# Small copies, minima and products placed on GpSimd, two-channel table products, dense products ahead of score steps, and plain first loads in a fused attention and state-space kernel

## The chip, the cores and the metric

The kernel runs on one core of a Trainium2 chip. The metric is the device time of one execution in microseconds (us); the median over the runs is compared. An execution that the hardware profiler recorded lies beside it: its span runs from the first to the last recorded instruction, and its own time is a little longer than its span.

## The reference, cut to what matters

```python
# A: 2048 tokens in 4 segments of 512, 32 heads of 16
q, k, v = x @ wq, x @ wk, x @ wv
for s in range(4):                                   # segment by segment
    p = softmax(qs @ ks.T / 4 + causal_mask)         # local attention
    a_mem = phi(qs) @ M / (phi(qs) @ z + 1e-6)       # phi(t) = t+1 if t>0 else exp(t)
    o = g * a_mem + (1 - g) * (p @ vs)
    M += phi(ks).T @ vs;  z += phi(ks).sum()
a = o @ wo
# B: a diagonal state-space convolution, 512 channels, 128 states
K[d, l] = Re(sum_n C[d,n] * exp(dt[d] * A[d,n] * l) * dt[d] * B[d,n])   # A, B, C complex
b = causal_convolution(x, K) + x * Dskip             # through FFTs in the reference
out = g_tok * a + (1 - g_tok) * b                    # g_tok = sigmoid(x . gate_w)
```

## The kernel before

Everything is recorded first as a list of operations with their readers and writers. A planner (`Sched.schedule`) then places them, engine by engine, with a cost for each operation and a priority (`key`, shifted for each group of operations by the table `ORDER`). Some operations, above all the evacuations of PSUM, may go to ScalarE or VectorE: the planner chooses, and the choice is fixed in the program. Each engine runs its list strictly in the order that comes out; waits are on semaphores. DMAs stand in SP's list, a few large ones in GpSimd's. All matmuls are issued from one helper (L820), all evacuations from another (ScalarE L324 and L327, VectorE L325 and L328), all DMAs from a third (L317).

**Part A, attention.** For each of 4 segments, `do_xT` brings the 512 tokens transposed into SBUF (DMA transposes); `project` makes q and k for 8 heads at a time (128 rows), evacuates them, makes a copy of k in which even heads are zeroed (`ko`, L1121), and, from the second segment on, phi(q): exp on ScalarE (L1125), then a minimum with 1, a maximum with 0, and a sum on VectorE (L1126 to L1128). `seg_state` does the same for k after a transpose on TensorE (exp L1075, maximum L1076, minimum L1077, sum L1078) and adds to the memory. `group` does 4 heads in five score steps: two or four matmuls write 1024 columns over two PSUM banks, ScalarE takes the exp of them (L1169, 160 times in all), and a matmul with v follows. The two bank pairs (0, 1) and (2, 3) are used in turn. The causal mask of a step is either added on TensorE (two matmuls with the identity) or multiplied in on VectorE after the exp (L1178); the table `MASKS` says which, bit by bit. `ophase` normalises (L1229 to L1252), sends the result through DRAM for a transpose, and `oproj` multiplies by wo.

**Part B, the convolution.** The kernel K is needed at 640 exponents, each a sum of one of 20 values (F) and one of 32 (G). `ssm_prep` makes exp(dt·A); `ssm_powers` squares it nine times in fp32, and at each of the 10 powers, for two halves of the channels, stores (re, im) in bf16, a negated im (L904) and a second copy of re (helper, 128x256). `tables(c)` builds F and G for 128 channels by complex products `cmul` (VectorE: L1328 and L1330 the two products, L1333 their sum), starting from five copies of 256 elements; `n` is the number of entries made at once, 1 to 8, so 256 to 2048 elements. It then multiplies G by F on TensorE channel by channel: 256 matmuls of 20 columns with 32-column weights for each c, 1024 in all, two evacuations of 320 elements for each c, and four small DMAs into the table KTT. `x_level1` makes the first step of the transform of x and stores it in DRAM (`scr_Z`).

**The tail.** 16 steps, each with 10 dense matmuls of KTT with a DFT matrix (loaded by GpSimd's queue), the second step of the transform of x, four VectorE operations for the complex product (L1425 to L1430), the way back, and a DMA into V2. It can begin only when the four tables are done, and the planner mixes it with the last groups of the attention. At the end 16 blocks of three matmuls, evacuated with the token gate (L327, L328), are written out.

**First loads.** SP issues six DMA transposes first (A_re, A_im, four parts of x), while ScalarE's queue issues the identity, log_dt, wq and wk.

Of the kernel before, what the change touches and what calls it, by code (L numbers as in the profile page):

```python
# [16 lines left out]
    'c_ident': (-302.654696, 118.5323), 'c_mk': (25.0776717, 31.1201), 'c_negm': (117.240337, 15.88946),  # L17
    'c_mask': (82.9696732, 148.73681), 'c_ones': (219.06097, 69.01982), 'c_W1': (101.972009, -1.91191),
    'c_G2': (152.510402, 64.12832), 'ld0': (-159.6066, -3.90904), 'ld1': (-178.483329, -24.17737),
    'ld2': (-92.104013, -32.87557), 'ld3': (-67.6677276, 9.94046), 'ld4': (-16.8975543, -9.33976),  # L20
    'ld5': (-4.87843354, -20.81767), 'ldt': (-255.221528, 18.97994), 'ldw0.3': (-120.015437, 20.25449),
    'ldw0.4': (-107.069287, 54.02795), 'ldw0.5': (-74.7706898, 55.68128), 'ldw50': (143.580885, 71.64248),
    'ldbd': (146.873282, -3.63178), 'ldc': (75.9548493, -139.44835), 'prep': (241.088944, 76.53782),
    'xT0': (-135.794939, 94.16918), 'powA0': (-118.34783, 47.94242), 'powA1': (293.056234, 56.59733),
    'powA2': (35.605867, 26.1545), 'powA3': (85.9672701, 3.55388), 'powA4': (-134.9878, 64.48103),
    'powA5': (-26.1625064, 59.29796), 'powA6': (-133.006553, -36.0664), 'powA7': (-142.410857, 92.25773),
    'powA8': (-143.096642, 54.65219), 'powA9': (-10.832777, 2.7911), 'cbA': (-135.566534, 76.23563),
    'powB0': (-38.6484402, 86.47076), 'powB1': (5.73197339, 19.09463), 'powB2': (-13.5842481, 50.52935),
    'powB3': (-134.626625, -55.3453), 'powB4': (-158.321758, -62.26012), 'powB5': (-189.375726, 81.95324),
    'powB6': (-80.3854645, -2.33938), 'powB7': (-23.5296877, 39.40937), 'powB8': (-69.1011372, 80.90111),  # L30
    'powB9': (-110.631611, 11.18354), 'cbB': (-43.7416241, -8.34436), 'gate0': (-83.6885532, -16.32166),
    'gate': (1.11235274, 54.68591), 'proj0.0': (-19.4170356, -12.54463), 'tok0': (-79.3938344, 28.87985),
    'state0': (2.03704365, 1.9988), 'grp0.0.0': (-9.77190791, 56.39033), 'grp0.0.1': (-15.5684214, 42.32006),
    'oph0.0': (16.6476846, 20.40017), 'proj0.1': (-31.4882721, 74.16452), 'grp0.1.0': (-22.0475879, 127.40729),
    'grp0.1.1': (-23.8762151, 61.87469), 'oph0.1': (-9.68776635, -98.76067), 'proj0.2': (13.8209713, 33.73148),
    'grp0.2.0': (-3.0729207, -42.9295), 'grp0.2.1': (-4.41502647, 85.93088), 'oph0.2': (-0.110628858, -73.44253),
    'proj0.3': (-3.65051527, 62.72309), 'grp0.3.0': (-157.898249, 69.86549), 'grp0.3.1': (15.8097506, 82.05476),
    'oph0.3': (1.58288994, 45.63335), 'oproj0': (-119.328043, -32.2024), 'xT1': (152.351944, 17.87594),
    'proj1.0': (9.25225381, 119.56925), 'tok1': (-10.2534902, 33.782), 'state1': (2.65910208, -104.20105),
    'grp1.0.0': (-90.77533, -81.81367), 'grp1.0.1': (2.11773201, -114.61486), 'oph1.0': (-2.73170943, -41.40325),  # L40
    'proj1.1': (1.88542876, 58.71674), 'grp1.1.0': (-50.654272, 32.17712), 'grp1.1.1': (2.9233842, 75.51506),
    'oph1.1': (-10.8350984, -95.48593), 'proj1.2': (1.82372045, 0.09674), 'grp1.2.0': (-40.190034, 101.48513),
    'grp1.2.1': (6.26606409, 118.92692), 'oph1.2': (-0.686318884, -116.61307), 'proj1.3': (0.240651948, 30.33776),
    'grp1.3.0': (-46.8631087, 31.58558), 'grp1.3.1': (4.26113506, 92.65595), 'oph1.3': (16.5142754, -29.00959),
    'oproj1': (-191.3713, -3.8356), 'xT2': (96.7803542, 126.17717), 'proj2.0': (2.03309827, 56.77169),
    'tok2': (4.1651971, -119.61949), 'state2': (5.77674239, -0.78865), 'grp2.0.0': (-34.2653109, -9.07765),
    'grp2.0.1': (-5.67836684, 97.22657), 'oph2.0': (-250.752907, -56.23876), 'proj2.1': (6.5976729, 122.63846),
    'grp2.1.0': (-4.50294478, 30.38303), 'grp2.1.1': (4.81855669, 106.57043), 'oph2.1': (15.6722872, -167.79793),
    'proj2.2': (-0.107249989, 90.02738), 'grp2.2.0': (-195.487509, 48.11696), 'grp2.2.1': (-5.26881311, 86.02262),
    'oph2.2': (10.7493513, -113.28868), 'proj2.3': (-7.49951321, 95.76044), 'grp2.3.0': (5.83724795, 81.21215),  # L50
    'grp2.3.1': (-32.6003357, 74.62712), 'oph2.3': (-34.0930078, -105.98926), 'oproj2': (-42.4160159, -7.99807),
    'xT3': (290.268696, 20.01374), 'proj3.0': (0.804501688, 7.58942), 'tok3': (5.05705523, 9.43832),
    'grp3.0.0': (-16.6209468, 115.71971), 'grp3.0.1': (-94.3400298, 75.95984), 'oph3.0': (34.3743725, -53.14357),
    'proj3.1': (-5.34871522, 74.39357), 'grp3.1.0': (31.8837621, -11.25205), 'grp3.1.1': (-311.171354, -14.40604),
    'oph3.1': (-107.203104, -69.86356), 'proj3.2': (72.9991952, 27.09956), 'grp3.2.0': (20.1657102, -6.85936),
    'grp3.2.1': (-59.0699755, -14.4919), 'oph3.2': (88.4879918, -147.86965), 'proj3.3': (79.119397, 97.40507),
    'grp3.3.0': (5.32990942, 126.86441), 'grp3.3.1': (61.7741135, -22.60438), 'oph3.3': (-130.287319, -60.50239),
    'oproj3': (-33.6345043, -45.3022), 'tab0': (-0.0762501383, 297.60803), 'tab1': (-3.85305439, 267.74954),
    'tab2': (-0.288638216, 266.94455), 'tab3': (9.72332812, 324.53498), 'xl1': (-134.058337, -22.9888),
    'tailload': (-94.6594205, 59.19368), 'K0': (-16.3376241, 5.32994), 'K1': (44.0845545, -26.15755),  # L60
    'K2': (9.34286849, 3.42233), 'K3': (45.356053, 32.70617), 'K4': (39.7158986, -80.36254),
    'K5': (59.226848, -13.36243), 'K6': (-175.798043, 23.12264), 'K7': (-52.4250027, -83.01271),
    'K8': (-81.0202091, -26.97997), 'K9': (70.2758069, 29.6753), 'K10': (11.2349379, 25.06385),
    'K11': (-5.3357892, -30.98575), 'K12': (-72.5533468, 4.35854), 'K13': (83.6417633, 0.11429),
    'K14': (94.4918388, -109.55134), 'K15': (132.562985, 53.83523), 'fin': (-85.9153477, -15.31372),
    'pre0': (169.976104, -25.42423), 'fin0': (91.9347751, 60.72191), 'pre1': (-73.3504102, -61.54381),
    'fin1': (115.799027, 117.99035), 'fin2': (125.104546, 66.48059), 'fin3': (213.962257, 170.74892),
}
MASKS = [2, 0, 0, 0, 0, 0, 0, 0, 0, 28, 0, 0, 0, 1, 0, 0, 16, 16, 14, 4, 0, 28, 0, 1, 3, 15, 31, 31, 15, 13, 26, 20]
# [122 lines left out]
class Sched:  # L192
# [141 lines left out]
    def schedule(self):  # L334
# [23 lines left out]
        dma_free = 4.5  # L358
# [221 lines left out]

def c_mm(n, k=1):
    return k * (0.014 + n / 2300.0)
# [53 lines left out]
def dft_const():  # L636
    lq = (np_bf16_bits(np.arange(2048, dtype=np.float32)).astype(np.uint32) << 16).view(np.float32).astype(np.int64)
    where = {}
    for f, fe in enumerate(F_EXP):
        for g, ge in enumerate(G_EXP):  # L640
            assert fe + ge not in where
            where[fe + ge] = (f % 5, 4 * g + f // 5)
# [14 lines left out]
def build_kernel(nc, A_x, A_wq, A_wk, A_wv, A_wo, A_beta, B_A_re, B_A_im, B_B_re, B_B_im,  # L657
                 B_C_re, B_C_im, B_log_dt, B_Dskip, gate_w, out):
    with contextlib.ExitStack() as es:
# [102 lines left out]
        kexP = mkpool("kex", 1280, 2)  # L762
# [3 lines left out]
        assert a <= 207 * 1024, a  # L766

        pbP = mkpool("pb", 1024, 2)
# [9 lines left out]
        pb2P = mkpool("pb2", 1024, 1, 0)  # L778
        a = GP.addr
        paP = mkpool("pa", 1024, 2, 0)  # L780
# [44 lines left out]
        for wi in range(6):  # L825
            T = Tile(paP if wi < 2 else pb1P if wi == 2 else pb2P if wi == 3 else pbP, BF16)
            S.tag = "ld%d" % wi
            S.dma(lambda T=T: ap(T, n=512), lambda wi=wi: bass.AP(prm[wi], 0, [[128, 512], [1, 128]]), 131072, w=[T], key=(-1.6, -1.7, 3.0, 3.1, 3.2, 3.3)[wi], tr=True)
            praw.append(T)
# [3 lines left out]
        for T, wsrc, ky in ((wqT, A_wq, 0.3), (wkT, A_wk, 0.4), (wvT, A_wv, 0.5), (woT, A_wo, 50.0)):  # L833
            S.tag = "ldw%g" % ky
            S.dma(lambda T=T: ap(T, dims=[[512, 4], [1, 512]]), lambda wsrc=wsrc: wsrc.rearrange("(k p) n -> p k n", p=128),
                  524288, w=[T], key=ky - 1.3 if ky < 1 else ky, early=ky < 0.45)
# [15 lines left out]
        def do_xT(s):  # L852
            S.tag = "xT%d" % s
            T = Tile(xTP, BF16)
            parts = []
            for k in range(4):
                S.dma(lambda T=T, k=k: ap(T, k * 512, n=512), lambda k=k: bass.AP(x.tensor, x.offset + s * 262144 + k * 128, [[512, 512], [1, 128]]),
                      131072, pw=[T], key=S.key - 8 if s else -1.5 + 0.1 * k, tr=True)
# [714 lines left out]
```

## Time and profile before

| what | value |
|---|---|
| median of 3 runs | 357.27 us (355.72 to 368.35) |
| the profiled execution's own time | 355.81 us |
| its span | 354.0 us |
| ScalarE busy | 285.9 us, of it 157.5 us the 160 exps |
| VectorE busy | 274.6 us, of it 101.4 us the table products (L1328, L1330, L1333) |
| TensorE busy | 298.4 us (ends of matmuls are modelled) |
| GpSimd busy | 17.3 us |
| mean granted TensorE clock | 0.946 of full speed |

In a row of the groups stand the line, engine and operation, then what is written and read with its shape, the count, the busy time and the mean of one, and the idle time of the engine just before. In a row of the stages stand, for each engine, busy time and number of instructions, then the granted clock, the busy share of the DMA engines and what they moved. "issue" as a releaser is time in which an engine waited for nothing that the profile shows. Lines of the changed file stand some 5 to 50 further down than those named here.

### The profile page before, as it was taken

Reading aid. Unit: us, or ns where it says so; the run is one execution under the profiler, and the core shown is the slowest. Engines: PE = TensorE matmul, PEld = TensorE weight load, DVE = VectorE, ACT = ScalarE, POOL = GpSimd, SP = SyncE. Lnnn points to the kernel's source line nnn. Section 1 sums busy time; section 2 is a strip of 40 time slices with the busy share of each in tenths; the row PEclk is TensorE's granted clock in tenths of the full one; section 3 lists DMA queues with packets and bytes.
Section 4 is the critical chain, followed back from the end, with each engine's and each line's share of the span. In section 5 each row is a group of like instructions: output and inputs, shape, how many; then the busy total and the mean of one; then the engine's idle time right before and its main releaser. Section 6 shows DMA issues by size and latency. Waiting matters only on the chain.

```text
span 354.0 us, 8296 instructions
## 1 busy us (share of the span) xinstructions
PE 298.4 (84%) x3409; PEld 125.1 (35%) x3409; DVE 274.6 (78%) x667; ACT 285.9 (81%) x387; POOL 17.3 (5%) x39
## 2 busy tenths in 40 slices
PE   0669887688939999999889999987999999999691
PEld 0223332233424432543335543353343333344240
DVE  2788999999848998399998899942877778986220
ACT  2798999899937998998999898945999768665472
POOL 2000000000000000000010000000001120100000
PEclk9996999699987996999999999998999999999897
DMA  7879021013592474801006210251134656533342
GB/s 173 172 161 109 1 91 30 3 54 99 197 148 76 136 176 126 205 23 30 2 8 186 71 44 17 59 167 37 40 102 181 217 181 211 149 114 93 109 156 90
DMA packets 43117, 37.56 MB, mean 106 GB/s; under 512 B 30568, under 2 KB 35944, under 8 KB 42216
## 3 DMA queue, kind: packets, MB, share of 16 engines
q1 hardware_dynamic: 39016, 22.18, 25.8%
q0 software_dynamic: 2720, 13.63, 12.3%
q10 hardware_dynamic: 1344, 1.21, 1.5%
q8 instruction: 27, 0.44, 0.5%
q14 instruction: 10, 0.08, 0.1%
HBM read 17.74 MB, written 9.44 MB: 77 GB/s over the span
## 4 chain that ended last, share of the span: by engine, by line
DVE 38%; PE 33%; ACT 20%; issue 4%; DMA 3%; SPq 0%
PE psum L820 33%; ACT sb L1169 11%; ACT sb L324 6%; DVE sb L1330 5%; DVE sb L1328 5%; DVE sb L1333 5%; DVE sb L325 4%; DMA sb<-in_B_A_im_dram 2%; ACT sb L327 2%; DVE sb L1232 2%; DVE sb L1252 1%; DVE sb L1178 1%; DVE sb L1430 1%; DVE sb L1425 1%; DMA sb<-sb 1%
## 5 line engine op out<-in xcount | busy, mean ns | idle before, releaser
L820 PE MATMUL psum<-sb 128*32 128x20 bf16 (+13 forms) x3233 | 287.7, 276 | 46.5 <-DMA sb<-in_A_x_dram 11.7
L820 PEld LDWEIGHTS psum<-sb 128*128 128x128 bf16 (+4 forms) x3233 | 115.0, 97 | 215.2 <-issue 88.4
L1169 ACT ACTIVATE sb<-psum 128x1024 bf16<-128x1024 f32 x160 | 157.5, 1037 | 7.7 <-PE psum L820 7.1
L324 ACT ACTIVATE sb<-psum 128x512 bf16<-128x512 f32 (+2 forms) x134 | 97.7, 753 | 37.6 <-PE psum L820 36.7
L325 DVE CAST sb<-psum 128x512 bf16<-128x512 f32 (+2 forms) x39 | 34.9, 894 | 16.0 <-PE psum L820 15.8
L1328 DVE TENSOR_TENSOR sb<-sb 128x512 bf16<-128x512 bf16 (+3 forms) x52 | 34.0, 657 | 0.1
L1333 DVE TENSOR_TENSOR sb<-sb 128x512 bf16<-128x512 bf16 (+3 forms) x52 | 33.8, 658 | 0.1
L1330 DVE TENSOR_TENSOR sb<-sb 128x512 bf16<-128x512 bf16 (+3 forms) x52 | 33.6, 658 | 0.0
L1178 DVE TENSOR_TENSOR sb<-sb 128x512 bf16<-128x512 bf16 (+1 forms) x43 | 15.6, 369 | 4.6 <-ACT sb L1169 4.4
L324 ACT ACTIVATE sb<-sb 128x256 bf16<-128x256 bf16 (+1 forms) x32 | 15.4, 500 | 1.1 <-DVE sb L904 1.0
L1425 DVE TENSOR_TENSOR sb<-sb 128x1024 bf16<-128x1024 bf16 x16 | 10.8, 683 | 6.5 <-ACT sb L324 5.2
L1430 DVE TENSOR_TENSOR sb<-sb 128x512 bf16<-128x512 bf16 x32 | 13.2, 417 | 0.6
L1229 DVE RECIPROCAL sb<-psum 128x32 f32<-128x32 bf16 x16 | 5.6, 350 | 10.4 <-PE psum L1226 10.4
L317 POOL DMA_DIRECT2D sb<-c_D x16 | 8.6, 538 | 91.4 <-PE psum L820 66.5
L327 ACT ACTIVATE sb<-psum,sb 128x512 bf16<-128x512 f32 x13 | 8.6, 687 | 4.7 <-PE psum L820 4.7
L1427 DVE TENSOR_TENSOR sb<-sb 128x1024 bf16<-128x1024 bf16 x16 | 10.9, 683 | 0.2 <-ACT sb L324 0.2
L1232 DVE TENSOR_TENSOR sb<-psum,sb 128x512 bf16<-128x512 bf16 x16 | 10.9, 682 | 0.0
L1226 PE MATMUL psum<-sb 128*128 128x128 bf16 x128 | 9.8, 220 | 0.1
L1252 DVE TENSOR_TENSOR sb<-psum,sb 128x256 bf16<-128x256 f32 x24 | 9.2, 415 | 0.1
L325 DVE COPY sb<-sb 128x256 bf16<-128x256 bf16 x17 | 3.9, 247 | 6.0 <-PE psum L820 6.0
L1226 PEld LDWEIGHTS psum<-sb 128*128 128x128 bf16 x128 | 7.5, 98 | 2.5 <-ACT sb L324 0.7
L1125 ACT ACTIVATE sb<-sb 128x512 bf16<-128x512 bf16 x12 | 8.0, 666 | 0.1
(71 smaller groups left out, 142.1 us busy)
## 6 DMA issues: line engine op xcount, KB each, us to landing
sb<-c_D POOLq DMA_DIRECT2D x16, 320.0 KB, 4.4
scr_Z<-sb SPq DMA_DIRECT2D x16, 256.0 KB, 2.0
sb<-scr_Z POOLq DMA_DIRECT2D x4, 1024.0 KB, 5.5
sb<-sb SPq DMA_DIRECT2D x15, 256.0 KB
sb<-in_A_x_dram POOLq DMA_DIRECT2D x4, 512.0 KB, 5.2
scr_obuf<-sb SPq DMA_DIRECT2D x12, 128.0 KB, 1.9
scr_abuf<-sb SPq DMA_DIRECT2D x12, 128.0 KB, 1.7
sb<-scr_abuf SPq DMA_DIRECT2D x3, 512.0 KB, 6.1
```

The costliest lines, as they stand in the source:

```text
L324: fa = lambda e: e.activation(dst(), src(), ACT.Copy)
L325: fd = lambda e: e.tensor_copy(dst(), src())
L327: fa = lambda e: e.activation(dst(), src(), ACT.Copy, scale=scale())
L820: mm = lambda e, o_, l, r_, st, sp, **kw: e.matmul(o_, lhsT=l, rhs=r_, start=st, stop=sp, skip_group_check=True, **kw)
L1169: op("ACT", c_act(1024), lambda e, P=P, pT=pT: e.activation(ap(pT, n=1024), ap(P, n=1024), ACT.Exp, scale=0.25), r=[P], w=[pT])
L1178: o_ = op("DVE", c_tt(128 * len(offs)), lambda e, pT=pT, dims=dims: e.tensor_tensor(ap(pT, dims=dims + [[1, 128]]), ap(pT, dims=dims + [[1 ...
L1226: i = e.transpose(ap(P, tb * 256 + gi * 128, n=128), ap(ra[gi], tb * 128, n=128), ap(ident, n=128))
L1232: op("DVE", c_dps(512), lambda e: e.tensor_tensor(ap(o1, dims=[[128, 4], [16, 8], [1, 16]]), ap(P, dims=[[256, 4], [32, 8], [1, 16]]), ap( ...
L1328: op("DVE", ct, lambda e: e.tensor_tensor(run(tile, ne, dst, 1), run(tile, ne, src, sstep), pwv(0), ALU.mult), r=rd + [pw], w=wr + [tile])
L1330: op("DVE", ct, lambda e: e.tensor_tensor(run(t2, n, 0, 1), run(tile, ne, src, sstep), pwv(1), ALU.mult), r=rd + [pw], w=[t2])
L1333: op("DVE", max(c_tt(256 * n), 0.4), lambda e: e.tensor_tensor(D_(), D_(), ap(t2, n * 128, [[-n * 128, 2], [2 * n, 64], [1, 2 * n]]), ALU. ...
L1430: op("DVE", c_tt(512), lambda e, Y=Y, Tt=Tt, c=c, alu=alu: e.tensor_tensor(ap(Y, 512 * c, n=512), ap(Y, 512 * c, n=512), ap(Tt, 512 * c, n ...
```

## The change

Five things are edited, and the priorities are replaced.

- **To GpSimd (POOL):** the negation and the copy of each power (20 and 20 of 256 elements); the five first copies of each table (20 of 256); the product L1330 wherever n is 1 or 2 (12 of 256 elements, 16 of 512); the masked k (16 of 512), the minimum for phi(k) (12 of 512), the minimum and the maximum for phi(q) (24 of 512). These are 140 instructions. In the before program the copies of 256 could go to either engine; all others were VectorE's.
- **Table products for two channels at once:** weights of 64 columns (two channels' G), 40 columns streamed (two channels' F), of which the two diagonal blocks are used: 512 matmuls in place of 1024. Twice as many elements are evacuated, in three pieces for each c (480, 480, 320). Each piece has its own priority and each set of 16 matmuls a later one. Channels therefore stand in another order, which the reads in `x_level1` and in the last products undo by a strided read of the streamed operand.
- **Dense products ahead of score steps:** where the new table `FILLS` has a bit (52 of 160 steps), a matmul of 128 rows by 512 columns into the step's bank comes first; its result is overwritten.
- **First loads:** A_re, A_im and the first segment of x come as they lie, and are transposed on TensorE (8 and 16 matmuls of 128 columns) and evacuated (two of 512, two of 1024). wq and wk are issued by SP behind them. ScalarE's queue issues the identity and log_dt alone.
- **Tables of the planner:** new `ORDER`; `MASKS` has 93 bits in place of 43, so 93 steps are masked on VectorE and 67 on TensorE (before: 43 and 117). Costs of the new GpSimd operations are added.

```diff
-op("DVE", c_ts4(512), lambda e: e.tensor_scalar_min(ap(ek, n=512), ap(ek, n=512), 1.0), w=[ek])
+op("POOL", c_pl(512), lambda e: e.tensor_scalar_min(ap(ek, n=512), ap(ek, n=512), 1.0), w=[ek])
...
-op("DVE", c_ts4(512), lambda e: e.tensor_scalar(ap(ko, n=512), ap(kT, n=512), ap(mkT, n=1), None, ALU.mult), r=[kT, mkT], w=[ko])
+op("POOL", c_pl(512), lambda e: e.tensor_scalar(ap(ko, n=512), ap(kT, n=512), ap(mkT, n=1), None, ALU.mult), r=[kT, mkT], w=[ko])
...
-op("DVE", ct, lambda e: e.tensor_tensor(run(t2, n, 0, 1), run(tile, ne, src, sstep), pwv(1), ALU.mult),
+op(*(("POOL", c_pl2(256 * n)) if n < 3 else ("DVE", ct)), lambda e: e.tensor_tensor(run(t2, n, 0, 1), run(tile, ne, src, sstep), pwv(1), ALU.mult),
    r=rd + [pw], w=[t2])
...
+if FILLS[gidx] >> si & 1:
+    mm(e, ap(P, n=512), ap(kT, n=128), ap(qT, n=512), True, True)
...
-for hf in range(2):
+for pc, (lo_, n_) in enumerate(((0, 12), (12, 12), (24, 8))):
...
-for dq in range(4):
-    dl = 32 * dq + 16 * hf + sl
-    i = mm(e, ap(P, sl * NF, n=NF, p0=32 * dq, np_=32), ap(G, (1 - cc) * GPL + (dl // 2) * 2 * NG + dl % 2, [[2, NG]]),
-           ap(F, cc * FPL + (dl // 2) * 2 * NF + dl % 2, [[2, NF]]), cc == 0, cc == 1, tile_position=(0, 32 * dq))
+for ct in range(2):
+    j, par = 32 * ct + (lo_ + sl) // 2 * 2, sl % 2
+    i = mm(e, ap(P, sl * 2 * NF, n=2 * NF, p0=64 * ct, np_=64), ap(G, (1 - cc) * GPL + j * 2 * NG + par, [[2, 2 * NG]]),
+           ap(F, cc * FPL + j * 2 * NF + par, [[2, 2 * NF]]), cc == 0, cc == 1, tile_position=(0, 64 * ct))
...
-i = mm(e, ap(P, hf * 512, n=512), ap(W1T, hf * 128, n=128), ap(xj, bl * 512, n=512), True, True)
+i = mm(e, ap(P, hf * 512, n=512), ap(W1T, hf * 128, n=128), ap(xj, bl * 512, [[2, 2], [4, 128], [1, 2]]), True, True)
...
-i = mm(e, ap(P, n=512), ap(G2T, kt * 128, n=128), ap(V2, (b4 * 2 + kt) * 512, n=512), False, kt == 1)
+i = mm(e, ap(P, n=512), ap(G2T, kt * 128, n=128), ap(V2, (b4 * 2 + kt) * 512, [[2, 128], [256, 2], [1, 2]]), False, kt == 1)
...
+if wi < 2:
+    S.dma(lambda T=T: ap(T, n=512), lambda wi=wi: prm[wi].rearrange("(p k) n -> p (k n)", k=4), 131072, w=[T], key=(-1.6, -1.7)[wi])
...
+    for t2 in range(2):
+        for k in range(4):
+            i = e.transpose(ap(P, t2 * 512 + k * 128, n=128), ap(xks, (2 * hb + t2) * 512 + k * 128, n=128), ap(ident, n=128))
```

## The prediction

> **What bounds the kernel now.** I read the busy times first, then the chain that ended last, then stages, and last the timeline where a stage looked odd.
>
> ```profile
> PE 298.4 (84%) x3409; PEld 125.1 (35%) x3409; DVE 274.6 (78%) x667; ACT 285.9 (81%) x387; POOL 17.3 (5%) x39
> ...
> DVE 38%; PE 33%; ACT 20%; issue 4%; DMA 3%; SPq 0%
> ```
>
> Three engines share the load almost evenly, the chain wanders among them, and GpSimd is empty. So relief of one engine alone would move the bound to the next.
>
> ```profile
> core 0: us, PE busy (x) PEld busy (x) DVE busy (x) ACT busy (x) POOL busy (x), PEclk, DMA share, GB/s
> 0.00:10.00 10.00, 0.00 (x0) 0.00 (x0) 2.13 (x5) 1.91 (x2) 1.89 (x9) 1.00 0.84 182
> ...
> 101.00:104.00 3.00, 0.00 (x0) 0.00 (x0) 0.00 (x0) 0.33 (x2) 0.00 (x0) 1.00 0.76 33
> 104.00:115.00 11.00, 10.18 (x59) 4.18 (x60) 8.42 (x19) 6.18 (x8) 0.00 (x0) 0.69 0.29 99
> ...
> 20.00:240.00 220.00, 190.08 (x2609) 82.34 (x2606) 193.67 (x496) 195.71 (x277) 7.84 (x16) 0.94 0.36 88
> 240.00:340.00 100.00, 93.70 (x744) 36.77 (x745) 69.40 (x144) 73.68 (x85) 7.53 (x14) 0.97 0.41 127
> ```
>
> Four stages: 11.7 us without a matmul; 20 to 240 us, where ScalarE (195.7) and VectorE (193.7) are both 88 to 89% busy; 240 to 340 us, where TensorE is (93.7 of 100); and an end of 14 us. Inside the second stage lie 3 us in which no engine works. The timeline there:
>
> ```profile
> 98.35 1.65 PE L820 MATMUL psum<-sb 128*32 128x20 bf16 x128 [0.49 <-issue]
> ...
> 104.82 1.48 PE L820 MATMUL psum<-sb 128*32 128x128 bf16 x10 [4.82 <-issue]
> ...
> 105.39 0.69 DVE L325 CAST sb<-psum 128x512 bf16<-128x512 f32 x1 [4.47 <-PE psum L820]
> ```
>
> 128 table matmuls go by in 1.65 us (13 ns each), then TensorE stops for 4.82 us on nothing that the profile shows. It happens again after a run of them at 237.5 us (3.14 us). Where they come in runs of 64 or fewer (145 to 150 us) it does not. My reading, an inference: instructions arrive by DMA (the page has a queue "instruction" with 27 packets of 16 KB), the runs use them faster than they come, and the DMA engines were 0.76 busy just then. The clock falls after it (0.69).
>
> [...]
>
> **The change part by part**, made against the profiled execution: span 354.0, own time 355.81, which is 1.5 below the median of the runs (357.27) and beside the lowest (355.72).
>
> *First loads.* A_im landed at 9.79 (2.04 + 7.75 in the chain), x at 11.7. Plain loads: ahead of x stand the identity, log_dt, A_re and A_im (0.42 MB), x is 0.5 MB, wq 0.5 MB. At the 182 GB/s of the first row these need 2.3, 5.2 and 8.1 us behind a start near 1.5; at the 300 GB/s of its best slices 1.4, 3.1 and 4.8. Four transposes and an evacuation (0.69, row L325) follow A_im, and log_dt was in use only at 5.25 before. So VectorE starts near 6 and the projections at 7 to 9.5, not 9.8 and 11.7: **-3.9**, between -2 and -4.5. It counts in full, as VectorE is 9 tenths busy from then on. Cover for wq's later place in SP's queue: the transposes of x; if it comes last, that is the 9.5.
>
> *ScalarE and VectorE.* Rows that leave:
>
> ```profile
> L324 ACT ACTIVATE sb<-sb 128x256 bf16<-128x256 bf16 x23 | 9.8, 448 | 1.1 <-DVE sb L904 1.0
> L1121 DVE TENSOR_SCALAR sb<-sb 128x512 bf16<-128x512 bf16 x16 | 5.4, 346 | 1.5 <-ACT sb L324 1.5
> L1330 DVE TENSOR_TENSOR sb<-sb 128x512 bf16<-128x512 bf16 x16 | 6.7, 420 | 0.0
> L1330 DVE TENSOR_TENSOR sb<-sb 128x256 bf16<-128x256 bf16 x12 | 4.8, 399 | 0.0
> L904 DVE TENSOR_SCALAR sb<-sb 128x256 bf16<-128x256 bf16 x20 | 4.2, 215 | 0.0
> L325 DVE COPY sb<-sb 128x256 bf16<-128x256 bf16 x17 | 3.9, 247 | 6.0 <-PE psum L820 6.0
> ```
>
> With L1077, L1126 and L1127 (12 each: 285, 318, 288 ns, 10.7 together) VectorE loses 35.7 and ScalarE 9.8. But by the order of the built programs VectorE gains: masks (43 to 93: 22 more of 285 ns, 28 more of 419 ns) 18.0; eight more evacuations of 1024 (1.219) 9.8; five of 512 (0.685) 3.4; the larger table pieces 3.1; four small ones 1.9. That is 36.2: **VectorE stays at 275**. ScalarE gives up in the same trade six of 1024 (1.028), three of 512 (0.617) and a few more, 10.4 together, so it falls by 20 to **266**. The sum of the two falls by 19.7; shared evenly that is **-9.5** in the middle stage, 0 if VectorE alone sets it.
>
> *TensorE.* 52 dense products cost 11.2 at 0.216; 50 steps fewer mask with two matmuls (56 of 256 columns, 44 of 128 leave), about -8.6 at the same price per column; table matmuls halve (12.0 us busy before; 0 to -6, since the wider weights may take longer); 24 transposes cost 1.5. Net about -2: **0**. The cover of a dense product is the exp of the other bank pair: 1.037 us, against 0.4 to 0.6 for a score step and 0.22 more. Without cover it costs its 11.2. Strided reads of the streamed operand: no row shows their price. 0 if they run at full rate; if at half, 64 x 0.216 = 14, 7 of it in the last blocks. I take 0: ScalarE and VectorE evacuate those blocks at 0.69 us for two engines, so only a part would show.
>
> *The stops.* Half the instructions, in pieces with exps between them, though runs of 96 and 80 stay. **-8** (4.8 and 3.1) is what I take; 0 if they stay, -12 if the slow clock behind them goes as well (8.7 us of TensorE alone on the chain from 104.8).
>
> *GpSimd.* 52 of 512, 60 of 256, and 28 products[...]. Room for it is there (11 to 240 us). But it is a queue in order: behind a k copy that waits for ScalarE stand products that VectorE waits for (L1333), the minima ahead of the memory update, and DMA issues of the tail's operands. Each chain gets longer: a small `cmul` was 0.4 + 0.4 + 0.4 on VectorE[...]. Other groups stand between, so 0 is its price in the sum if the order is kept, one to three at worst near the tables' end. Contention: some 160 us of VectorE's work in the middle stage has two SBUF inputs. [...] I take **+6**[...].
>
> Sum: -3.9 - 9.5 - 8 + 6 = -15.4, so 355.8 - 15.4 = **340.4 us**.
>
> **Rivals.** *Contention decides.* [...] VectorE, already 88% busy and with no less work, becomes the bound. [...] Against it: nothing measured. It outweighs the gains of 21.4 from a stretch of 0.15 us for each of 140 instructions on; at a quarter of a microsecond, 35, the time is 370. *The freed time goes idle.* VectorE is as loaded as before and its table chains pass through a queue, the stops stay since DMA traffic is the cause: only the first loads count, 350 to 354. For it: VectorE's unchanged 275. *All of it comes.* No contention, and the slow clock goes: 355.8 - 3.9 - 9.5 - 12 - 3 [...] = 327.
>
> **How the numbers follow.** Forecast (333 to 348) 0.50; all of it 0.13; idle 0.17; contention 0.20. The likeliest gives 340.4, its own range 333 to 348. Leaving out a little below 326 and most of the contention case, the range is 326 to 366. Faster by over 2% (below 348.7 by the profiled execution), about the least that a measurement of this kernel can tell from no change: 0.63; within: 0.17; slower: 0.20.
>
> **What would show it.** The first matmul before 10 us; no gap on "issue" over 1 us in TensorE's waits; ScalarE near 266 and VectorE near 275 busy. VectorE well above 275, with the same forms longer than before (420 ns for a product of 512), means contention; rows L1333 or score steps waiting for GpSimd mean that its queue decides; last blocks whose matmuls lie over 0.3 us apart mean the strided reads. Wrong would be, above all, a GpSimd instruction that holds VectorE up for its whole length.

## The result, and the profile after

The median is 389.93 us (387.75 to 392.93), beside 356.50 us of the kernel before. The ratio is 1.098 (95% interval 1.085 to 1.110): slower, outside the predicted range of 326 to 366. The profiled execution took 387.75 us, its span is 385.8. Line numbers are those of the changed file; L1376, L1378 and L1381 are the table products and their sum (L1328, L1330 and L1333 before), L330 an evacuation (or another copy by the same helper) on VectorE.

The page of the changed kernel, busy times and the chain by engine:

```profile
PE 318.3 (83%) x2873; PEld 131.6 (34%) x2873; DVE 314.9 (82%) x621; ACT 272.5 (71%) x351; POOL 185.2 (48%) x179
...
DVE 37%; PE 30%; POOL 15%; ACT 9%; issue 4%; DMA 3%; SPq 0%; DVEq 0%; ACTq 0%
```

VectorE has 46 instructions less than before and is busy for 40 us more. GpSimd is at 185 us, of them 170 for the 140 instructions (116 by the planner's costs), and holds 15% of the chain, on which it did not stand before. TensorE has 536 matmuls less and is busy for 20 us more, at a granted clock of 0.904 in place of 0.946.

The stages again, with the same columns (the last one is longer here, from 240 to 372 us in place of 240 to 340):

```profile
0.00:10.00 10.00, 2.95 (x25) 2.60 (x26) 4.93 (x10) 4.60 (x6) 1.87 (x9) 1.00 0.88 203
20.00:240.00 220.00, 176.27 (x1734) 73.70 (x1733) 199.16 (x395) 161.37 (x215) 156.75 (x144) 0.87 0.27 74
240.00:372.00 132.00, 122.77 (x1062) 49.25 (x1060) 103.11 (x202) 93.81 (x114) 22.70 (x24) 0.95 0.38 114
```

The start is better: 2.95 us of matmuls in the first 10 us, none before. From 20 to 240 us VectorE is busier than before (199.2 us, 193.7 before), although 106 of the 496 instructions that it executed there have moved to GpSimd (it executes 395 now). ScalarE falls from 195.7 to 161.4 us there, more than it has lost in work (13 us over the whole span), so part of its work has slid behind 240 us. The granted clock falls from 0.94 to 0.87. That stage is where the time goes.

VectorE's groups by shape show the first reason. Before:

```profile
L1328 DVE TENSOR_TENSOR sb<-sb 128x512 bf16<-128x512 bf16 x16 | 6.6, 410 | 0.0
...
L325 DVE CAST sb<-psum 128x1024 bf16<-128x1024 f32 x16 | 19.5, 1219 | 4.7 <-PE psum L820 4.6
```

After:

```profile
L1376 DVE TENSOR_TENSOR sb<-sb 128x512 bf16<-128x512 bf16 x16 | 10.8, 675 | 0.0
...
L330 DVE CAST sb<-psum 128x1024 bf16<-128x1024 f32 x24 | 28.9, 1216 | 2.6 <-PE psum L833 2.5
```

A product of 512 took 410 ns before and takes 675 now; 256 elements went from 406 to 543, the sum of 512 from 415 to 564. Not all rows grow alike: the masks of 512, two inputs in SBUF too, went from 419 to 454, products of 2048 from 1212 to some 1260. What comes from PSUM takes what it took (1216 ns, 1219 before). So the rows that grew are of instructions whose operands are all in SBUF; not every such row did (a reciprocal of 32 columns takes 346 ns, 348 before).

GpSimd's groups, same columns:

```profile
L1165 POOL TENSOR_SCALAR sb<-sb 128x512 bf16<-128x512 bf16 x16 | 29.7, 1858 | 17.1 <-ACT sb L329 16.8 <-DVE sb L330 0.2
L1121 POOL TENSOR_SCALAR sb<-sb 128x512 bf16<-128x512 bf16 x12 | 21.9, 1826 | 13.7 <-ACT sb L1119 13.7
...
L1378 POOL TENSOR_TENSOR sb<-sb 128x512 bf16<-128x512 bf16 x16 | 20.5, 1283 | 12.6 <-DVE sb L1381 12.6
```

One input of 512 takes 1.6 to 1.9 us, up to twice the 0.97 with which the planner placed it (`c_pl(512)`); two inputs of 512 take 1.28, about as planned (1.33). So the queue runs later than its plan. The waits (time, times, longest) and a piece of the chain in order of time show it:

```profile
DVE sb L1122 <- POOL sb L1121: 5.9, 3, 5.2
DVE sb L1172 <- POOL sb L1171: 5.0, 5, 1.5
```

```profile
94.12 1.75 POOL sb L1171
95.87 7.68 POOL sb L1388 x4
103.55 1.53 POOL sb L1165
```

From 92 to 107 us the chain runs through GpSimd alone: a maximum and a minimum, then four table copies, a masked k, a product and another minimum, each behind the one ahead in its queue. Of the 7.68 us of the four copies, one alone takes 5.18; the median of the 16 such copies is 0.59. While it lasts, VectorE executes SBUF-to-SBUF products one behind the other at their usual length (1.21 us), and the copy ends soon after the first VectorE instruction that reads PSUM (some of the products between are left out):

```profile
95.82 5.18 POOL L1388 COPY sb<-sb 128x256 bf16<-128x256 bf16 x1
...
97.01 1.21 DVE L1381 TENSOR_TENSOR sb<-sb 128x2048 bf16<-128x2048 bf16 x1
98.14 1.21 DVE L1376 TENSOR_TENSOR sb<-sb 128x2048 bf16<-128x2048 bf16 x1
...
100.62 0.41 DVE L1120 TENSOR_SCALAR sb<-psum 128x512 bf16<-128x512 bf16 x1
```

So the holding up seems to go both ways, and GpSimd's queue is late for two reasons: its instructions are slower than planned even at their shortest (1.48 us for one input of 512), and some of them are drawn out beside VectorE's. If each took the shortest time of its row, the 140 would take 137 us in place of 170, an estimate from this trace.

So there are two suspects, both of one edit: VectorE's instructions get longer, and GpSimd's queue is late. "Contention" stands below for the first of them.

### The profile page after: what moved, and what is told of

Same layout as the page of the kernel before. It is cut to its first block, busy times and chain, and to the rows that moved or that the text cites. A ratio compares the mean times of both kernels' runs of the same rounds, so it can differ in the third digit from the quotient of the medians.

```text
span 385.8 us, 7303 instructions
## 1 busy us (share of the span) xinstructions
PE 318.3 (83%) x2873; PEld 131.6 (34%) x2873; DVE 314.9 (82%) x621; ACT 272.5 (71%) x351; POOL 185.2 (48%) x179
## 4 chain that ended last, share of the span: by engine, by line
DVE 37%; PE 30%; POOL 15%; ACT 9%; issue 4%; DMA 3%; SPq 0%; DVEq 0%; ACTq 0%
PE psum L833 28%; DVE sb L330 6%; DVE sb L1376 5%; ACT sb L1217 5%; DVE sb L1381 5%; POOL sb L1165 4%; DVE sb L1226 4%; ACT sb L329 3%; DVE sb L1378 3%; POOL sb L1121 3%; POOL sb L1388 2%; DMA sb<-sb 2%; POOL sb L948 2%; DVE sb L1280 1%; DVE sb L957 1%
## 5 line engine op out<-in xcount | busy, mean ns | idle before, releaser
L833 PE MATMUL psum<-sb 128*128 128x512 bf16 (+18 forms) x2673 | 305.1, 310 | 54.1 <-DVE sb L1226 12.1
L833 PEld LDWEIGHTS psum<-sb 128*128 128x128 bf16 (+5 forms) x2673 | 117.4, 104 | 235.4 <-issue 86.1
L329 ACT ACTIVATE sb<-psum 128x512 bf16<-128x512 f32 (+4 forms) x124 | 89.6, 741 | 61.0 <-PE psum L833 57.7
L330 DVE CAST sb<-psum 128x512 bf16<-128x512 f32 (+3 forms) x56 | 49.9, 899 | 17.2 <-PE psum L833 17.0
L1376 DVE TENSOR_TENSOR sb<-sb 128x512 bf16<-128x512 bf16 (+3 forms) x52 | 40.8, 790 | 0.2
L1226 DVE TENSOR_TENSOR sb<-sb 128x512 bf16<-128x512 bf16 (+1 forms) x93 | 37.8, 414 | 2.8 <-ACT sb L1217 2.7
L1381 DVE TENSOR_TENSOR sb<-sb 128x512 bf16<-128x512 bf16 (+3 forms) x52 | 38.5, 742 | 0.5 <-POOL sb L1378 0.2
L1165 POOL TENSOR_SCALAR sb<-sb 128x512 bf16<-128x512 bf16 x16 | 29.7, 1858 | 17.1 <-ACT sb L329 16.8
L1378 POOL TENSOR_TENSOR sb<-sb 128x512 bf16<-128x512 bf16 (+1 forms) x28 | 29.6, 1063 | 15.1 <-DVE sb L1381 14.8
L1170 POOL TENSOR_SCALAR sb<-sb 128x512 bf16<-128x512 bf16 x12 | 20.2, 1685 | 20.4 <-ACT sb L329 20.2
L1121 POOL TENSOR_SCALAR sb<-sb 128x512 bf16<-128x512 bf16 x12 | 21.9, 1826 | 13.7 <-ACT sb L1119 13.7
L1378 DVE TENSOR_TENSOR sb<-sb 128x1024 bf16<-128x1024 bf16 (+1 forms) x24 | 24.5, 1025 | 0.0
L1171 POOL TENSOR_SCALAR sb<-sb 128x512 bf16<-128x512 bf16 x12 | 18.8, 1564 | 8.3 <-ACT sb L1169 8.3
L1388 POOL COPY sb<-sb 128x256 bf16<-128x256 bf16 x16 | 14.4, 937 | 0.1
L949 POOL COPY sb<-sb 128x256 bf16<-128x256 bf16 x20 | 12.1, 607 | 1.2
```

Source lines behind the costliest of these rows:

```text
L329: fa = lambda e: e.activation(dst(), src(), ACT.Copy)
L330: fd = lambda e: e.tensor_copy(dst(), src())
L833: mm = lambda e, o_, l, r_, st, sp, **kw: e.matmul(o_, lhsT=l, rhs=r_, start=st, stop=sp, skip_group_check=True, **kw)
L1121: op("POOL", c_pl(512), lambda e: e.tensor_scalar_min(ap(ek, n=512), ap(ek, n=512), 1.0), w=[ek])
L1165: op("POOL", c_pl(512), lambda e: e.tensor_scalar(ap(ko, n=512), ap(kT, n=512), ap(mkT, n=1), None, ALU.mult), r=[kT, mkT], w=[ko])
L1226: o_ = op("DVE", c_tt(128 * len(offs)), lambda e, pT=pT, dims=dims: e.tensor_tensor(ap(pT, dims=dims + [[1, 128]]), ap(pT, dims=dims + [[1 ...
```

## The experiments

Medians in us; the ratio is to the kernel before, run on the same chip in turn; busy times are those of the profiled execution.

| run | median | ratio (95%) | VectorE | GpSimd |
|---|---|---|---|---|
| changed kernel | 389.93 | 1.098 (1.085 to 1.110) | 314.9 | 185.2 |
| GpSimd's instructions cut | 346.54 | 0.970 (0.960 to 0.979) | 285.1 | 102.0 |
| before, and GpSimd busy beside | 400.97 | 1.112 (1.095 to 1.129) | 309.3 | 197.7 |
| no dense products | 390.75 | 1.092 (1.083 to 1.101) | 316.1 | 182.0 |
| contiguous reads | 387.81 | 1.084 (1.074 to 1.094) | 315.3 | 181.9 |
| late queue alone | 380.21 | 1.065 (1.057 to 1.073) | 287.1 | 187.7 |
| same order, work on VectorE | 367.50 | 1.027 (1.014 to 1.040) | 307.2 | 17.3 |
| cut, on VectorE | 347.07 | 0.967 (0.958 to 0.976) | 292.3 | 22.1 |
| the same, contention alone | 401.37 | 1.118 (1.110 to 1.127) | 337.1 | 195.2 |
| the same, with fills | 352.33 | 0.985 (0.971 to 0.999) | 299.1 | 125.6 |
| without the GpSimd edit, planned anew | 361.63 | 1.014 (0.999 to 1.029) | 293.3 | 17.2 |
| another such plan | 360.59 | none formed | 292.8 | 17.6 |
| GpSimd planned with true durations | 398.63 | 1.116 (1.105 to 1.127) | 313.1 | 181.9 |
| before, half of the table matmuls | 349.72 | 0.980 (0.976 to 0.984) | 274.4 | 17.3 |
| before, plain loads untransposed | 354.60 | 1.002 (0.995 to 1.009) | 274.9 | 17.2 |
| two-channel tables alone | 350.39 | 0.985 (0.976 to 0.993) | 292.5 | 17.4 |

### Is it GpSimd at all? Its instructions cut, the plan kept

```diff
-e.tensor_scalar_min(ap(ek, n=512), ap(ek, n=512), 1.0)
+e.tensor_scalar_min(ap(ek, n=4), ap(ek, n=4), 1.0)
```

and so on for 118 of the 140; the planner still sees the old costs, so every engine keeps its order.

> The changed kernel with its whole plan kept, but 118 of the 140 moved GpSimd instructions handle 2 or 4 columns in place of 256 or 512 (22 first uses stay whole), so the rest of those columns is not computed; four fills at the start stand in for it. Waits and order stay. Theory A (what the GpSimd instructions take, as a late queue and as contention, is the whole loss): VectorE's busy time falls from 315 to about 280, products of 512 take 420 ns again, and the time is about 340 us (332 to 350), where the prediction put it. Rival B (the loss lies in the rest: 50 more masks on VectorE, the dense products, the strided reads, the new order): it stays over 370 us though VectorE's instructions are short again.

```profile
PE 298.9 (86%) x2840; PEld 127.4 (37%) x2873; DVE 285.1 (82%) x621; ACT 270.7 (78%) x351; POOL 102.0 (29%) x183
```

346.5 us, and products of 512 back at 413 to 470 ns. Theory A: 43 us go with the length of GpSimd's instructions, and the 50 further masks on VectorE, the dense products and the strided reads are all still in. B is out. VectorE at 285 and GpSimd at 102 show that some contention is left, so this is no clean zero.

### Contention alone, in the order of before

140 operations are put into GpSimd's list, each behind one exp, reading and writing the unused `rT` pool (turned through three outputs; kinds mixed evenly; `o` is the exp).

```diff
+p.alld = [o] + ([m] if i < 3 else [dm[i - 3]])
+p.fn = lambda e, n=n, d=i % 3 * 512: e.tensor_scalar_min(A(512 + d, n), A(0, n), 1.0)
```

> The kernel before, in its own order, with 140 further GpSimd instructions on scratch (52 minima of 512, 60 of 256, 16 products of 512, 12 of 256), each let go by one exp; nothing waits for them. So this is contention alone. Theory C (contention is most of the loss): VectorE goes from 275 to over 300 busy, its products of 512 from 420 to over 500 ns, and the time from 356 to 380 or more. Rival Q (the late queue is most of it): VectorE's forms lengthen, but the time stays within 10 us of the kernel before (356 to 366).

```profile
PE 329.2 (82%) x3382; PEld 133.9 (34%) x3409; DVE 309.3 (77%) x667; ACT 292.6 (73%) x387; POOL 197.7 (49%) x180
```

401 us: 41 more than before, although no row of the waits names one of the added instructions as what an engine waited for. VectorE goes from 274.6 to 309.3 with the same 667 instructions. TensorE goes from 298.4 to 329.2 with its own unchanged work: it stands still for 70 us of the span in place of 56, and its granted clock is 0.83 to 0.86 in the four runs, 0.946 before. Whether the standing still brings the lower clock, no run here separates. Theory C holds here.

### Dense products and strided reads

```diff
-if FILLS[gidx] >> si & 1:
-    mm(e, ap(P, n=512), ap(kT, n=128), ap(qT, n=512), True, True)
```

> The changed kernel, plan kept, with the 52 dense products left out (they were overwritten anyway). The prediction: they are hidden under the exps, so 390 stays 390 (within 3 us). Rival: without cover they lie on the path, and up to 52 x 0.216 = 11 us are gained, about 379.

390.75 us: nothing gained. The dense products are hidden, as forecast.

```diff
-ap(V2, (b4 * 2 + kt) * 512, [[2, 128], [256, 2], [1, 2]])
+ap(V2, (b4 * 2 + kt) * 512, n=512)
```

and likewise for the first transform of x.

> The changed kernel, plan kept, with the streamed operand of the last blocks and of the first transform read as it lies (512 elements in a row) in place of 2x2x128 and 128x2x2; the channels then come out in another order. The prediction took 0 for the strided reads: 390 stays within 2 us. Rival, half rate: the last blocks' matmuls go from 0.30 to 0.22 us and up to 7 us go at the end, about 383.

387.8 us, 2 below, which is inside the scatter of the runs. The timelines of TensorE's last run of matmuls, before and after (start, length), show the price more plainly:

```profile
337.14 9.24 PE L820 MATMUL psum<-sb 128*128 128x512 bf16 x42 [1.44 <-DMA sb<-sb]
```

```profile
365.74 12.54 PE L833 MATMUL psum<-sb 128*128 128x512 bf16 x42 [2.30 <-DMA sb<-sb]
```

0.22 us each before, 0.30 in the mean now. The same run of matmuls in two stretches, with the columns of the stages, shows what the mean is made of:

```profile
365.74:369.92 4.18, 4.18 (x11) 1.43 (x12) 0.75 (x1) 1.38 (x2) 0.00 (x0) 0.52 0.00 0
369.92:378.20 8.28, 8.28 (x33) 3.02 (x31) 2.25 (x3) 6.13 (x9) 0.00 (x0) 1.00 0.53 198
```

In the first stretch the granted clock is at half (0.52), and from start to start a matmul takes 0.42 to 0.43 us, read in strides or not. In the second, at the full clock, those that read in strides take 0.27 and the others 0.22, as all did before. Read contiguously, the first 12 take 4.05 us and the other 29 take 6.66, 0.23 each, at a mean clock of 0.83. So the strided reads cost 1.2 us at the end (7.9 us for 31 matmuls, 6.7 at 0.216 each, the spacing from start to start in this run of matmuls before), worked out from the starts in the trace, and nothing shows while the clock is at half. The other 2.0 us of the difference to before go with the half clock: the mean there was 1.00 before and is 0.84 now. In the two cut runs this stretch of matmuls lasts 12.5 and 12.6 us, at 0.82 and 0.83.

### The late queue alone

The cut run again, but each cut instruction is followed by 2 to 4 instructions of 4 columns on scratch before it signals:

```diff
+def more(e, fn=o.fn, k=k, at=seen):
+    fn(e)
+    for j in range(k):
+        i = e.tensor_scalar_min(A(8 + 4 * (at + j)), A(0), 1.0)
+    return i
```

> As the run with the cut GpSimd instructions (346.5 us), but each cut instruction is followed by 2 to 4 further ones of 4 columns on scratch before it lets go what waits for it. So GpSimd's queue is about as long as in the changed kernel, while hardly any data passes between it and SBUF: the late queue without the contention. Theory C (contention is the loss): VectorE's forms stay short (products of 512 under 480 ns), VectorE near 285, and the time within 10 us of 346.5 (to 357). Rival Q (the late queue is a good part of it): 362 or more, with VectorE and TensorE waiting for GpSimd as in the changed kernel (3 to 6 us a line).

```profile
PE 318.8 (84%) x2840; PEld 132.6 (35%) x2873; DVE 287.1 (76%) x621; ACT 273.7 (72%) x351; POOL 187.7 (50%) x544
```

```profile
DVE sb L1161 <- POOL sb L487: 10.8, 5, 4.7
```

380.2 us. VectorE's instructions are as short as in the cut run (287.1 busy), yet 34 us are lost: VectorE waits 10.8 us for the minima of phi(k) alone (L1161 is the sum behind them), the sums of phi(q) 5.2, and TensorE 5.8 for the masked k. So theory C in the form "the queue costs little" is wrong. A late queue by itself can cost most of what the change lost. These waits are longer than those of the changed kernel (5.9, 5.0 and 3.1 us for the same three), so the 34 may be more than the queue's share there.

### The same work, the same order, on VectorE

```diff
+for o in order:
+    if o.eng == "POOL" and not o.dma and o.cost != 0.6:
+        o.eng = "DVE"
```

> The changed kernel's order on every engine, with the 140 moved instructions executed by VectorE at the place in time where the planner had them on GpSimd. By the rows of the kernel before they take 42 us there (52 at 0.31, 20 at 0.215, 40 at 0.247, 16 at 0.42, 12 at 0.40), so VectorE is near 320 busy, about what contention makes it in the changed kernel (315). Theory C (GpSimd takes from VectorE as much time as it saves it): within 10 us of 390. Rival Q (waiting for a slow queue is what costs): 372 or less, as nothing waits for GpSimd any more.

```profile
PE 303.1 (83%) x2840; PEld 128.3 (35%) x2873; DVE 307.2 (84%) x761; ACT 272.7 (75%) x351; POOL 17.3 (5%) x39
```

367.5 us, 22 below the changed kernel, and the rows of the 140 instructions sum to 42.0 us (5.6 for the masked k, 10.7 for the minima and maxima, 8.7 for the powers, 5.6 for the table copies, 11.4 for the products). So VectorE's other work is 307.2 - 42.0 = 265.2. In the changed kernel the same other work takes 314.9. **Freed of 42.0 us, VectorE loses 49.7 to GpSimd's company**, 0.355 us for each instruction taken away. Against the kernel before it is still 2.7% slower: with all of the work back on it, VectorE is at 307 us in this order. Rival Q has the time right (372 or less), theory C the busy times.

### Contention alone, in the order of the changed kernel

First the base: the cut instructions, executed by VectorE. Then the same with 140 whole instructions on scratch on GpSimd, each let go by what let go the original (the last line of the diff is in the second run alone).

```diff
+if o.eng == "POOL" and not o.dma and o.cost not in (0.6, 0.0):
+    o.eng = "DVE"
+    res.append(self.full(o, len(dm), [dm[-3]] if len(dm) > 2 else pws_))
```

> The base of the next run: the changed kernel's order, with 118 of the 140 moved instructions cut to 2 or 4 columns (the rest of those columns isn't computed) and all 140 executed by VectorE, so nothing waits for GpSimd and it does nothing beside. [...] VectorE: 280 to 295 busy, 346 to 360 us.

> The same, and GpSimd executes 140 whole instructions of the same kinds, on scratch, let go by what let go the original ones; nothing waits for them. So contention alone in the changed kernel's order. Theory C (contention alone is as bad here as it was in the order of before, +41): 25 us or more over its base. Rival Q (the late queue is the main loss of the changed kernel, 34 alone, and contention adds about 10): 15 us or less over its base, though VectorE's forms lengthen as in the changed kernel (by 30 us or more in sum).

The base (347.1 us): its busy times, and products of 2 columns.

```profile
PE 291.3 (85%) x2840; PEld 124.7 (36%) x2873; DVE 292.3 (85%) x761; ACT 271.7 (79%) x351; POOL 22.1 (6%) x44
```

```profile
L1423 DVE TENSOR_TENSOR sb<-sb 128x2 bf16<-128x2 bf16 x21 | 3.1, 150 | 0.0
```

With GpSimd beside (401.4 us): the same two rows.

```profile
PE 325.0 (81%) x2840; PEld 134.5 (34%) x2873; DVE 337.1 (85%) x761; ACT 274.7 (69%) x351; POOL 195.2 (49%) x184
```

```profile
L1425 DVE TENSOR_TENSOR sb<-sb 128x2 bf16<-128x2 bf16 x21 | 8.6, 408 | 0.0
```

54 us more, with nothing waiting for GpSimd. Theory C holds, by more than expected. The row of 2 columns tells how: a product with two elements a row to read takes 408 ns in place of 150. So the loss is not in proportion to the data; it looks like a wait that a VectorE instruction may meet: of the 761, 166 are over 0.1 us longer than the median of their form in the base, the longest by 0.97. A piece of the timeline of this run shows one:

```profile
60.79 1.14 POOL L517 TENSOR_TENSOR sb<-sb 128x512 bf16<-128x512 bf16 x1 [3.72 <-DVE sb L1428]
60.95 1.26 DVE L1425 TENSOR_TENSOR sb<-sb 128x512 bf16<-128x512 bf16 x1
```

VectorE's product starts 0.16 us into GpSimd's and ends 0.28 us after it; alone it takes 0.42. Others that overlap are only a little longer (a mask of 512 at 62.13 us took 0.61, 0.42 in the base), so not every meeting costs the whole length. The mean is 44.8 us of VectorE over 140 instructions, 0.32 each. TensorE pays too: it is busy for 34 us more, at a granted clock of 0.865 in place of 0.962.

### Does a better plan help?

The changed kernel without the GpSimd edit and without dense products (the placements of before are put back), against GpSimd with costs near the true ones; each with a new ORDER and MASKS. The diff is the second's cost of one input, `c_pl`.

```diff
-    return 0.2 + 0.0015 * n
+    return 0.3 + 0.0027 * n
```

> The changed kernel with the 140 instructions back where the kernel before had them (VectorE, the 60 copies that may go to ScalarE chosen by the planner) and without dense products, planned anew (other ORDER and MASKS): first loads and two-channel tables remain of the change. Both theories: no contention and no queue, so it gains on the kernel before what the first loads (-4), the stops (-8) and the plan bring: about 346 (340 to 352). Over 354 would mean that the rest of the change brings nothing.

> The changed kernel with its 140 instructions on GpSimd, without dense products, planned anew with costs near the measured ones (1.68 us for one input of 512, 0.99 of 256, products as before), so the planner works around the slow queue. Rival Q (a queue planned too short is the loss): about as fast as the run without GpSimd (within 8 us). Theory C (contention is enough for the loss, +54 alone in the order of the changed kernel): 25 us or more over it, 372 or more, with VectorE's products of 512 over 480 ns.

The second: busy times, the largest wait of VectorE for GpSimd, and the products of 512.

```profile
PE 324.5 (82%) x2849; PEld 136.8 (35%) x2873; DVE 313.1 (79%) x599; ACT 271.1 (69%) x347; POOL 181.9 (46%) x179
```

```profile
DVE sb L1325 <- POOL sb L1322: 2.6, 1, 2.6
...
L1320 DVE TENSOR_TENSOR sb<-sb 128x512 bf16<-128x512 bf16 x16 | 11.5, 726 | 0.1
```

361.6 and 398.6 us. With the true durations in the plan the waits for GpSimd all but vanish (2.6 us), and it is as slow as ever, 37 us over the run without GpSimd; its products of 512 take 726 ns. The two have different plans, so the 37 is not a clean difference. But with the run of contention alone it shows which cause is the larger: the late queue is enough for a loss, and without it the loss stays. Contention is the cause that this plan did not take away.

### What collides?

```diff
-p.fn = lambda e: e.tensor_scalar_min(A(d, n), A(0, n), 1.0)
+p.fn = lambda e: e.memset(bass.AP(v.tensor, v.offset + self.scr // 2, [[v.ap[0][0], 128], [1, 2 * n]]), 1.0)
```

> As the contention run (401 us; its base without GpSimd 347), but GpSimd's 140 instructions are fills of scratch (4 KB or 2 KB a row), which read nothing and last about 1.0 and 0.6 us. If it is the reading of two streams from SBUF that collides with VectorE, nothing is lost: 347 to 352, VectorE near 292. If any GpSimd instruction with SBUF holds VectorE up, by its time: about 110 us of fills against 174 us of the others, so 54 x 110/174 = 34 more, about 380.

```profile
L515 POOL MEMSET sb<- 128x1024 f32 x68 | 65.7, 967 | 89.7 <-ACT sb L329 34.2 <-ACT sb L1162 20.4 <-DVE sb L1424 16.4
```

```profile
L1421 DVE TENSOR_TENSOR sb<-sb 128x2 bf16<-128x2 bf16 x21 | 3.1, 150 | 0.0
...
L1164 DVE TENSOR_SCALAR sb<-sb 128x4 bf16<-128x4 bf16 x12 | 6.1, 507 | 0.0
```

In the base the last row was:

```profile
L1166 DVE TENSOR_SCALAR sb<-sb 128x4 bf16<-128x4 bf16 x12 | 1.9, 160 | 0.0
```

352.3 us, 5 above the base, with VectorE busy for 7 us more (45 more beside instructions that read). The table products keep their time beside fills (2 columns 150 ns, 512 columns 410 to 422; masks of 256 rise a little, 279 to 314), but one-input instructions do not (4 columns: 507 ns, 160 in the base; 512 columns of the masked k: 707, 349). So fills, which only write, hold up one kind of instruction above all (a sum of 512, two inputs, rose from 417 to 464). That points to GpSimd's reading as what holds up the products, which are the bulk of VectorE's work here; a GpSimd instruction that reads and writes nothing was not tried.

### What the rest of the change is worth

> The same edit as the run without GpSimd (361.6 us), with another ORDER and MASKS that the planner rates alike. If that plan was unlucky: 345 to 352. If the rest of the change brings nothing whatever the plan: 357 to 364.

The median is 360.6 us, but the four runs are 359.9, 361.3, 363.1 and 350.5: three where "nothing whatever the plan" has it and one where "unlucky" has it, so this run decides nothing. The first plan's 1.014 (0.999 to 1.029) stands alone: first loads and tables together brought nothing there that shows. Two runs in the order of before take them apart:

```diff
-for cc in range(2):
+for cc in range(1):
```

> The kernel before, order kept, with the second half of each table sum left out: 512 table matmuls of 13 ns instead of 1024, in runs of at most 64. The prediction's step: the stops on nothing (4.8 and 3.1 us) go, and the time falls by 8 (5 to 10). Rival: the stops go or shrink, but what comes after waits for something else, and the time falls by less than 3.

0.980 (0.976 to 0.984): 7 us, about what was forecast for the stops. Of them one of 2.2 us is left (8.5 in sum before; this profile is of the longest of the six runs, 355.0 us). But fewer matmuls are also less work, as the rows of the table matmuls show, before and here:

```profile
L820 PE MATMUL psum<-sb 128*32 128x20 bf16 x1024 | 12.0, 176 | 4.0 <-issue 3.6 <-DVE sb L1333 0.2
...
L820 PE MATMUL psum<-sb 128*32 128x20 bf16 x512 | 7.0, 177 | 0.2 <-DVE sb L1333 0.2
```

5 us of TensorE's own time go with the stops, and this run cannot tell the two apart. The last run below can, in part.

```diff
+if s == 0:
+    o.fn = lambda e, T=T, k=k: e.dma_start(ap(T, k * 512, n=512), bass.AP(x.tensor, x.offset + k * 65536, [[512, 128], [1, 512]]))
```

and likewise for A_re and A_im.

> The kernel before, order kept, with A_re, A_im and the first segment of x loaded as they lie into the same tiles, not transposed at all (so other numbers are computed from them). Nothing else moves. The prediction's step: VectorE starts near 6 and the projections before 10 us, and all of it counts, -3.9 (-2 to -4.5). Rival: the start is earlier, but the end isn't: 0 to -1.

1.002 (0.995 to 1.009): nothing. But this run only half tests the step. VectorE's own work started at 7.45 in place of 9.79 us and gained nothing at the end; the first matmul still waited 11.4 us for x, as wq and wk went ahead of x in ScalarE's queue, which the change alters as well.

> The kernel before with the two-channel tables alone (and the strided reads that undo their order), planned anew with 58 to 70 masks on VectorE; first loads, placements and dense products as before. The prediction's step of the stops: they go and 5 to 10 us with them, 347 to 352. Rival: TensorE's stops go, but the larger table pieces and the masks on VectorE (285 or more, 275 before) take it back: 355 to 362.

```profile
PE 298.3 (85%) x2846; PEld 124.0 (36%) x2871; DVE 292.5 (84%) x705; ACT 277.1 (79%) x366; POOL 17.4 (5%) x39
```

350.4 us, 0.985 (0.976 to 0.993): 1.5% below the kernel before. No stop of TensorE over 0.3 us is left, although VectorE is busy for 18 us more than before. And the table matmuls take as long as before (11.7 us, 12.0 before), so here it is not less work of theirs that pays:

```profile
L768 PE MATMUL psum<-sb 128*64 128x40 bf16 x512 | 11.7, 188 | 0.8 <-DVE sb L1281 0.7
```

The plan is new as well, so that the stops are the reason is likely, not shown. Two-channel tables are the one part of the change for which a gain was measured, and it comes without the rest. Why the plans with the first loads on top are some 10 us slower in all of their runs but one is open: each of the three has its own ORDER and MASKS, and I can't tell the edit from the plan.

## Why the prediction was wrong, step by step

- **GpSimd, "I take +6": the step that failed.** Contention alone costs 54 in the order of the changed kernel and 41 in that of before. The +6 was an estimate of mine: I took it that the two engines seldom get in each other's way, and had no measured number for it. A product of 2 columns went from 150 to 408 ns, so even the smallest product loses a quarter of a microsecond in the mean. Which instructions suffer, the traces show: a product of 512 with both inputs in SBUF takes 675 ns in place of 410, an evacuation of 1024 from PSUM 1216 and 1219. That contention might come was named; how it comes, by what looks like waits (the longest 0.97 us), and how much it costs I had wrong.
- **GpSimd, "0 is its price in the sum if the order is kept".** A late queue alone cost 34. The 140 instructions took 170 us where the planner's costs sum to 116, since one input of 512 takes 1.6 to 1.9 us and not 0.97, and even the shortest here, 1.48, is far over that. The kernel before had only fills and DMA issues on GpSimd, so no trace that I had showed their length. The order was kept; the times were not, and in a queue in order the difference adds up.
- **The rival "contention decides" had the cause and was too small.** A quarter of a microsecond each, 35 us, was to give 370. Measured are 0.25 each in the order of before, 0.32 and 0.355 in that of the changed kernel, 35 to 50 us of VectorE; and the time rises by more than VectorE's (41 for 35, 54 for 45); TensorE runs at a lower clock besides (0.865 in place of 0.962), which may be the rest. Its break-even of 0.15 us an instruction was passed by far. With VectorE already 88% busy and nothing measured on either side, two in ten was too little.
- **The two losses do not add.** 34 and 54 apart are 43 together (389.9 against 346.5). An argument, not shown: while VectorE waits for a late minimum it can't be held up by contention, and the instructions that it lacks can't be stretched.
- **VectorE "stays at 275", ScalarE 266.** Without contention VectorE's other work is 265.2, ten less than worked out; ScalarE is at 272.5, six more. The exchange of work was read about right (half of its 19.7 is 9.9, not 9.5), but VectorE was not spared what it gave away: 42.0 given, 49.7 taken.
- **The stops, -8.** Near in size in the order of before (7, of which the halved work may be a part), and gone in the changed kernel (no row of the waits of its matmuls names "issue" there). That instructions come late was an inference, and no run shows it. In the sum it was lost behind GpSimd.
- **First loads, -3.9.** The first projection starts at 9.79, not between 7 and 9.5 (11.7 before), VectorE at 6.94, not 6. That "it counts in full" is not confirmed: VectorE's earlier start alone brought nothing (1.002).
- **TensorE, net 0.** Dense products 0: right; -8.6 for the masks is -8.4 by its own price. Strided reads: taken at 0, they cost 1.2 in the last blocks, of the 7 that I had as the other bound there. The sign that I named for them, last blocks over 0.3 us apart, came true for a stretch at half clock, where they cost nothing that shows: it would have misled.

## What to carry to other kernels

Before giving VectorE's small elementwise work to an idle GpSimd, compare what the instruction takes on VectorE (here 0.30 us in the mean) with what its company costs there (here 0.25 to 0.36 for each): where VectorE works mostly from SBUF to SBUF and is near its bound, nothing was freed. Then multiply the planned length of a queue in order by what a first run shows: an engine that is half idle can still be on the chain (here 48% busy, 15% of the chain). A mean can hide such a hold-up: look at the longest of a row as well as its mean (here 5.18 us in a row with a median of 0.59). And of a change in several parts, try each part alone, since here the one that paid was hidden under the one that lost.

## What the runs showed of the hardware that I had not expected

- On GpSimd a tensor-scalar operation is slower than a product of two tensors: 1.56 to 1.86 us against 1.28 for 512 bf16 elements, 1.05 against 0.77 for 256; a plain copy of 256 takes 0.61. These are means beside a busy VectorE; the shortest of each show the same (1.48 and 1.08, 0.84 and 0.68, 0.40). With 4 columns one takes 0.33 us, back to back. VectorE takes 0.29 to 0.35 us for the same 512.
- VectorE's one-input instructions (bf16) are held up even by GpSimd's fills: 4 columns take 160 ns in the base, 507 beside them, while products of 2 columns keep their 150.
- A GpSimd copy of 256 elements lasted 5.18 us beside a row of VectorE's products that kept their 1.21 us, and ended as that row was broken by an instruction that reads PSUM (one case).
- A matmul of 512 columns that streams pairs of elements from strided places took 0.27 us at the full granted clock, a contiguous one 0.22; at half clock both took 0.42 to 0.43.
